# A spectral filter and MLP kernel on one Trainium2 core: compact stage-1 matrices, V reordered first, batch 0's products on three engines, double-matrix blocks for batch 1

## Chip, cores and metric

One core of one Trainium2 chip. The metric is the device time of one execution in microseconds (us); lower is better. Ratios below are of runs in the fast state alone, beside runs of the kernel before on the same chip. Fast runs of one kernel scatter by up to 1.3% (553.67 to 560.84 us for the kernel before in the last rounds), so differences under half a per cent are read with their intervals. The moments inside a kernel come from one profile each.

## The reference

Eight batches of 3136 tokens with 256 channels. A filter over the sequence in the frequency domain, then low-rank token mixing, then an MLP over the channels with a residual:

```python
X = np.fft.rfft(x, axis=1)                        # x: (8, 3136, 256)
y = np.fft.irfft(X * (filt_r + 1j * filt_i), n=3136, axis=1)
# ... y becomes the x of the second part
h = xt @ U @ V                                    # xt = y.transpose(0, 2, 1); U: 3136x32, V: 32x3136
u = y + h.transpose(0, 2, 1)
out = u + np.maximum(u @ w_ch1, 0.0) @ w_ch2      # w_ch1: 256x1024, w_ch2: 1024x256
```

## The kernel before

The transform is factored as 3136 = 64 x 49. **Stage 1** multiplies by 64-point matrices with the twiddles in them (`wf`), **stage 2** by 49-point matrices (`w2t`), then comes the **filter product**, **stage 3** goes back over 49 points (`g3`), and **stage 4** back over 64 points to tokens. Stage 4 has 32 more rows for the low-rank term: V's rows in `sv[64:96]`, and the sum over U's spectrum `uh` copied into `e2[64:96]` by `put_h`. Between stages 1 and 2 and between stages 3 and 4 the data changes its partition axis by a write to and a read from device memory (`ct1`, `ct2`).

TensorE then runs the MLP in groups of 512 tokens, eight steps to a group. The stages 1 to 3 of batch b+1 are laid between these steps by a plan. The **low-rank step** of a batch below is `low_rank(b)`, the sum that `put_h` needs; an **eviction** is the copy of a result out of PSUM, where TensorE leaves it, into SBUF. Only batch 0 has nobody to hide behind. The parts concerned:

```python
wf = cst.tile([128, 25, 128], F16, name="wf")        # two 64-column matrices per block, mostly zeros
# ...
for a in range(0, NK, 8):
    load_filters(a, a + 8)                           # issued by GpSimd
# ...
nc.gpsimd.dma_start(vnat, moe_V)
nc.gpsimd.dma_start(w1sb, ...)

def u_hat():                                         # U's spectrum, on VectorE
    # ...
        for f in range(2):
            nc.vector.tensor_mul(t[f]..., z[...], free(tw, ...))      # z is PSUM
        nc.vector.tensor_add(uh[:, :, p:p + 8], t[0], t[1])           # both inputs in SBUF

def mid_first():                                     # batch 0, stages 2 and 3
    # ...
    for j in range(16):
        # ... stage 2 with w2t and w2t's turned copy: "double-matrix" form, one product instead of three
        if j in (7, 9, 12, 14):
            nc.scalar.copy(pc, pz); nc.gpsimd.tensor_mul(uv, pc, fin)
        else:
            nc.vector.tensor_mul(uv, pz, fin)

def make_fa(i):                                      # filter copies for the later batches' form
    s = slice(8 * i, 8 * i + 8)
    nc.scalar.copy(fc[0:64, s], fb[64:128, s])
    nc.vector.tensor_scalar_mul(fc[64:128, s], fb[64:128, s], -1.0)
    nc.vector.tensor_copy(fa[64:128, s], fb[0:64, s])
    # ...

mid_first()
load_e2(0, 0); load_e2(0, 1)                         # reads of stage 4's input, issued by SyncE
nc.gpsimd.tensor_copy(sv[64:96, :]..., vnat...)      # V reordered
low_rank(0)                                          # 32 matmuls in four column strips
for n, _ in enumerate(st1(1)): ...                   # all 13 pieces of batch 1's stage 1
keep_warm(6)                                         # fillers
stage4(groups[0], 0); stage4(groups[0], 1)
# ...
at(4, x_after, 2)                                    # x loads of batch 2, held until a ReLU of group 0
# ...
m = later(start[b - 1], (5, -9, -12)[min(b, 3) - 1])
z = plan_mid(b, m, (2, 5) if b > 1 else (1, 3, 5))   # blocks whose three products GpSimd does
```

Of the kernel before, what the change touches and what calls it, by code (L numbers as in the profile page):

```python
# [16 lines left out]
NK = 32  # L17
# [7 lines left out]
def _consts():  # L25
# [10 lines left out]
    wf = np.zeros((128, 25, 128))  # L36
    for h in range(2):
        wf[h::2, 0:24, 64 * h:64 * h + 64] = t1[:, 24 * h:24 * h + 24]
    wf[0:64, 24, 0:64] = t1[:, 48]
# [59 lines left out]
    return (wf.reshape(128, 25 * 128).astype(f16), w2.astype(f16), g3.astype(f16),  # L99
# [4 lines left out]
def kernel(  # L104
# [48 lines left out]
    wf = cst.tile([128, 25, 128], F16, name="wf")  # L153
    for c in range(4):
        i = slice(8 * c, min(8 * c + 8, 25))
        nc.sync.dma_start(wf[:, i], wf_d.rearrange("p (i m) -> p i m", m=128)[:, i])
# [47 lines left out]
    usb = hflat[0:64, 0:NR * RANK]  # L204
    nc.gpsimd.dma_start(usb, moe_U.rearrange("(q r) p -> q (r p)", q=NQ))
# [3 lines left out]
    make_identity(nc, idn)  # L209

# [7 lines left out]
    nc.scalar.dma_start(g3, g3_d.rearrange("p (f m) -> p f m", f=6))  # L218

# [4 lines left out]
    vnat = hflat[64:96, 4704:4704 + SEQ]  # L224
    nc.gpsimd.dma_start(vnat, moe_V)
    nc.gpsimd.dma_start(w1sb, moe_w_ch1.rearrange("(h dd) c -> dd h c", h=2))

    sv = cst.tile([96, SEQ], F16, name="sv")
    kr = cst.tile([128, 96], F16, name="kr")

    def keep_warm(n):
        z = bank("f")
        for _ in range(n):
            nc.tensor.matmul(z, wf[:, 0, :], wf[:, 0:4, :].rearrange("p i m -> p (i m)"),
                             start=True, stop=True)
# [4 lines left out]
    def u_hat():  # L240
        ud = hflat[0:64, 1568:4704].rearrange("q (p c r) -> q p c r", c=2, r=NR)
# [18 lines left out]
    def st1(b):  # L260
# [22 lines left out]
        nc.tensor.matmul(pf[0:64, 0:DM], wf[0:64, 24, 0:64], xt[b, 3], start=True, stop=True)  # L283
# [11 lines left out]
    def turned(c):  # L295
        for g in range(0, 8 if c < 3 else 1, 4):
            for hh in range(2):
                z = bank("f")
                n, o = 512, 3136 * hh + (8 * c + g) * 128
                if c < 3:  # L300
                    for i in range(4):
                        nc.tensor.matmul(z[:, 128 * i:128 * i + 128],
                                         xt[0, c][:, (g + i) // 2, DM * (i % 2) + 128 * hh:DM * (i % 2) + 128 * hh + 128],
                                         wf[:, 8 * c + g + i, :], start=(i == 0), stop=True,
                                         skip_group_check=True)
                else:
                    n = 64
                    nc.tensor.matmul(z[:, 0:n], xt[0, 3][:, 128 * hh:128 * hh + 128],
                                     wf[0:64, 24, 0:64], start=True, stop=True)
# [6 lines left out]
    esb = {}  # L316
# [6 lines left out]
    def out3(b, k, half, pe):  # L323
        if half == 0:
            esb[b, k] = sb.tile([98, 4, DM], F16, tag="esb", bufs=10, name="esb")
        nc.scalar.copy(esb[b, k][:, 2 * half:2 * half + 2, :].rearrange("p s d -> p (s d)"),  # L326
                       pe[0:98])
        if half:
# [25 lines left out]
    def mid_first():  # L354
# [18 lines left out]
        todo = []  # L373

        def do3(j, uv):
            pe = bank("e0")
            stage3(pe, [(uv[:, 0], 2, 4), (uv[:, 1], 3, 5)], j == 15)
            out3(0, j // 2, j % 2, pe)

        for k in range(4):  # L380
            turn_a2(k)
        for c in range(4):
            load_x(1, c)
        nc.gpsimd.dma_start(w2sb, moe_w_ch2.rearrange("(cc t) e -> cc (t e)", t=8))
        for j in range(16):
# [7 lines left out]
            if j in (7, 9, 12, 14):  # L393
# [3 lines left out]
                nc.gpsimd.tensor_mul(uv, pc, fin)  # L397
            else:
                uv = sb.tile([128, 2, 2 * DM], F16, tag="ta", bufs=3, name="uv")
                nc.vector.tensor_mul(uv, pz, fin)  # L400
            if j < 4:
                turn_a2(j + 4)
            todo.append((j, uv))
            if len(todo) > 3:
                do3(*todo.pop(0))
        while todo:
            do3(*todo.pop(0))


    h1 = {}  # L410
# [21 lines left out]
    def load_e2(b, c):  # L432
# [5 lines left out]
        nc.sync.dma_start(t[0:64], dram(ct2[b], 8 * c * DM, [[NR * DM, 64], [1, n * DM]]))  # L438
# [19 lines left out]
    def stage4(gr, dh):  # L458
# [23 lines left out]
        nc.vector.tensor_copy(o, v)  # L482
# [58 lines left out]
    def make_fa(i):  # L541
        s = slice(8 * i, 8 * i + 8)
        nc.scalar.copy(fc[0:64, s], fb[64:128, s])
        nc.vector.tensor_scalar_mul(fc[64:128, s], fb[64:128, s], -1.0)
        nc.vector.tensor_copy(fa[64:128, s], fb[0:64, s])
        if i == 3:
# [7 lines left out]
    for c in range(4):  # L554
        turned(c)
        keep_warm(2)
    nc.sync.dma_start(sv[0:64], s4_d)
    nc.sync.dma_start(kr, kr_d)
    mid_first()
    load_e2(0, 0)  # L560
    load_e2(0, 1)
    nc.gpsimd.tensor_copy(sv[64:96, :].rearrange("p (r q) -> p r q", q=NQ),
                          vnat.rearrange("p (q r) -> p r q", q=64))
    low_rank(0)
    for n, _ in enumerate(st1(1)):
        if n == 3:
            low_rank_end(0)
        if n == 6:
            put_h(0, 0)
    load_e2(0, 2)  # L570
    load_e2(0, 6)
    keep_warm(6)
    stage4(groups[0], 0)
    stage4(groups[0], 1)
    for c in (1, 2, 6):
        put_h(0, c)
    make_fa(0)
    make_fa(1)


# [29 lines left out]
    def plan_mid(b, s, on_pool):  # L610
# [36 lines left out]

        lead = (4, 8, 9)[min(b, 3) - 1]
# [3 lines left out]
        for k in range(8):  # L652
            at(s, two, k)
            if k + 3 < 8:
                at(s, fetch, k + 3)
            if k in on_pool:
# [4 lines left out]
            else:  # L661
# [5 lines left out]
                d = max(later(s, 5), end)  # L667
# [29 lines left out]
    gens = {}  # L697

    def step1(b):
        if b not in gens:  # L700
            gens[b] = st1(b)
        next(gens[b])

    for c in range(3, 6):
        at(8 * c - 14, load_e2, 0, c)
    at(1, make_fa, 2)
    at(3, make_fa, 3)
# [7 lines left out]
    for b in range(1, NB):  # L715
# [4 lines left out]
        m = later(start[b - 1], (5, -9, -12)[min(b, 3) - 1])  # L720
        z = plan_mid(b, m, (2, 5) if b > 1 else (1, 3, 5))
# [46 lines left out]
```

## Time and profile before

555.93 us (median of 3, 555.91 to 557.05); profiled span 555.2 us.

| marker in the profile before | us |
|---|---|
| first filter product | 25.1 |
| last stage-3 eviction of batch 0 | 49.1 |
| first stage 4 / first MLP matmul of group 0 | 59.5 / 61.2 |
| first MLP matmul of group 1 | 72.0 |
| low-rank step of batch 1 | 121.1 |
| low-rank step of batch 2 | 183.3 |

Later batches follow about every 61 us. The time can therefore be split at three markers: the **start** (to group 1), the **middle** (group 1 to batch 1's low-rank step), the **handoff** (from there to batch 2's low-rank step). A change there moves the end by as much.

Five lines of the timeline of the kernel before will be needed (start, length, engine, line, operation, output and input, count, idle before and its releaser; SPq is SyncE issuing transfers):

```profile
12.48 0.42 DVE L257 TENSOR_TENSOR uh<-ut 98x256 f16<-98x256 f32 x1
...
47.44 6.95 POOL L562 COPY sv<-hring 32x3136 f16<-32x3136 f16 x1
...
59.59 1.05 SPq L286 DMA_DIRECT2D ct<-al  x1
...
66.92 0.60 PE L352 MATMUL psum<-a,w2t 98*128 98x512 f16 x2
67.02 4.25 POOL L170 DMA_DIRECT2D x<-in_x_dram  x6 [0.33 <-POOL x L168]
```

Read them as an order of events. U's adds (0.42 us) are long over when GpSimd reorders V. Batch 1's last stage-1 write (`al`) goes out at 59.6 us, its first stage-2 block runs at 66.9 without a wait, and the x loads of batch 2 start only after that.

### The profile page before, as it was taken

The numbers are of one execution on the slowest core, as the hardware profiler recorded it, in microseconds if no ns is written. First come the engines' busy times: TensorE is split into PE (matmuls) and PEld (weight loads), VectorE is DVE, ScalarE is ACT, GpSimd is POOL, SyncE is SP. The second block draws the span as 40 slices with busy tenths as digits, with TensorE's granted clock in tenths as the row PEclk, the third lists the DMA queues.
The fourth block names the chain that finished last, engine by engine and source line by source line (L and its number), as shares of the span: only waits on it lengthen the run. The fifth ranks groups of instructions, "written<-read, shape, count | busy, mean of one in ns | idle before, by whom it ended". The sixth has DMA issues, their size and how long they took to land.

```text
span 555.2 us, 11638 instructions
## 1 busy us (share of the span) xinstructions
PE 517.2 (93%) x4491; PEld 375.3 (68%) x4491; DVE 353.1 (64%) x409; ACT 390.8 (70%) x684; POOL 282.4 (51%) x194
## 2 busy tenths in 40 slices
PE   5976689997999999999999999999999999999996
PEld 2634356664767777777776777777786777777775
DVE  6764675755756686758846785858746887643332
ACT  8566868774777688767776788677777577765663
POOL 5778179951883165915683175806563297300000
PEclk9999899997999999999999999999999999999999
DMA  9998876894669468774879468865653553333212
GB/s 194 157 170 192 225 141 187 209 230 130 174 184 250 125 176 199 173 204 137 193 222 221 123 173 228 166 199 152 186 170 121 141 167 121 106 113 115 96 77 87
DMA packets 85432, 92.06 MB, mean 166 GB/s; under 512 B 6741, under 2 KB 69416, under 8 KB 85376
## 3 DMA queue, kind: packets, MB, share of 16 engines
q1 hardware_dynamic: 67968, 75.12, 45.5%
q0 software_dynamic: 16960, 15.91, 19.1%
q8 instruction: 35, 0.57, 0.4%
q10 hardware_dynamic: 448, 0.28, 0.3%
q14 instruction: 21, 0.17, 0.1%
HBM read 57.42 MB, written 49.77 MB: 193 GB/s over the span
## 4 chain that ended last, share of the span: by engine, by line
PE 70%; POOL 10%; DVE 7%; DMA 6%; ACT 4%; issue 2%; DVEq 0%; ACTq 0%; POOLq 0%; SPq 0%
PE psum L521 25%; PE psum L488 24%; PE psum L352 4%; PE psum L344 4%; PE psum L477 4%; PE psum L497 3%; PE psum L266 3%; POOL y L634 3%; DMA x<-in_x_dram 3%; POOL x L170 2%; DVE ut L482 1%; DVE tb L632 1%; PE psum L416 1%; DMA w1sb<-in_moe_w_ch_dram 1%; ACT asb L273 1%
## 5 line engine op out<-in xcount | busy, mean ns | idle before, releaser
L492 ACT ACTIVATE hring<-psum 128x512 f16<-128x512 f32 (+1 forms) x416 | 237.7, 576 | 104.5 <-PE psum L488 103.2
L488 PE MATMUL psum<-ut,w1sb 128*128 128x512 f16 (+1 forms) x832 | 240.3, 370 | 6.4 <-ACT hring L492 3.0
L521 PE MATMUL psum<-w2sb,hring 128*128 128x256 f16 x1536 | 230.9, 273 | 0.0
L634 POOL TENSOR_TENSOR y<-ta,tb 128x1024 f16<-128x1024 f16 x56 | 120.5, 2159 | 159.4 <-DVE tb L632 115.5
L521 PEld LDWEIGHTS <-hring 128*128 128x128 f16 x1536 | 143.3, 98 | 63.8 <-issue 3.8
L482 DVE CAST ut<-psum 128x512 f16<-128x512 f32 x96 | 71.1, 741 | 108.3 <-PE psum L477 88.2
L488 PEld LDWEIGHTS <-w1sb 128*128 128x128 f16 x832 | 104.6, 145 | 27.3 <-issue 10.4
L529 DVE COPY och<-psum 128x512 f32<-128x512 f32 x96 | 66.2, 689 | 47.3 <-PE psum L497 46.6
L326 ACT CAST esb<-psum 98x512 f16<-98x512 f32 x128 | 74.7, 586 | 21.6 <-PE psum L344 16.0
L628 DVE TENSOR_TENSOR ta<-psum,fb 128x1024 f16<-128x1024 f32 x41 | 50.0, 1218 | 7.9 <-PE psum L352 6.9
L273 ACT CAST asb<-psum 128x512 f16<-128x512 f32 x78 | 45.7, 589 | 12.3 <-PE psum L266 11.2
L497 PE MATMUL psum<-idn,ut 128*128 128x128 f16 x392 | 54.0, 220 | 0.0
L477 PEld LDWEIGHTS <-e 96*128 96x128 f16 x768 | 35.9, 99 | 25.5 <-issue 10.2
L630 DVE TENSOR_TENSOR tb<-psum,fc 64x1024 f16<-64x1024 f32 x41 | 50.3, 1226 | 0.9
L632 DVE TENSOR_TENSOR tb<-psum,fc 64x1024 f16<-64x1024 f32 x41 | 49.9, 1218 | 0.8
L477 PE MATMUL psum<-sv,e 96*128 96x64 f16 x768 | 38.8, 194 | 6.5 <-DMA e<-ct 3.7
L344 PE MATMUL psum<-y,g 128*98 128x512 f16 x105 | 39.9, 380 | 3.0 <-POOL y L634 1.5
L497 PEld LDWEIGHTS <-ut 128*128 128x128 f16 x392 | 38.4, 98 | 4.9
L628 POOL TENSOR_TENSOR ta<-pc,fb 128x1024 f16<-128x1024 f16 x15 | 32.4, 2159 | 10.7 <-ACT pc L638 10.7
L352 PE MATMUL psum<-a,w2t 98*128 98x512 f16 x113 | 34.3, 379 | 1.7 <-DVE tb L632 1.6
L266 PE MATMUL psum<-x,wf 128*128 128x256 f16 x168 | 31.3, 274 | 2.8 <-DVE asb L271 1.0
L630 POOL TENSOR_TENSOR tb<-pc,fc 64x1024 f16<-64x1024 f16 x15 | 31.8, 2122 | 1.2
(93 smaller groups left out, 373.6 us busy)
## 6 DMA issues: line engine op xcount, KB each, us to landing
out_dram<-och SPq DMA_DIRECT2D x47, 512.0 KB
ct<-esb SPq DMA_DIRECT2D x64, 196.0 KB
x<-in_x_dram POOLq DMA_DIRECT2D x48, 256.0 KB, 8.1
e<-ct SPq DMA_DIRECT2D x48, 256.0 KB
a<-ct SPq DMA_DIRECT2D x56, 196.0 KB
ct<-asb SPq DMA_DIRECT2D x42, 256.0 KB
wf<-wf SPq DMA_DIRECT2D x3, 256.0 KB
w1sb<-in_moe_w_ch_dram POOLq DMA_DIRECT2D x1, 512.0 KB, 6.8
```

Source lines behind the costliest of these rows:

```text
L326: nc.scalar.copy(esb[b, k][:, 2 * half:2 * half + 2, :].rearrange("p s d -> p (s d)"), pe[0:98])
L344: nc.tensor.matmul(pe[0:98], g3[:, m, :], v, start=(n == 0), stop=(n == len(parts) - 1))
L477: nc.tensor.matmul(pu[:, 64 * i:64 * i + 64], e2[b, c][:, i, 128 * dh:128 * dh + 128], sv[:, 64 * r:64 * r + 64], start=(i == 0), stop=Tru ...
L482: nc.vector.tensor_copy(o, v)
L488: nc.tensor.matmul(ph[:, 0:n], w1sb[:, dh, :, t], gr.ut[:, dh, 0:n], start=(dh == 0), stop=(dh == 1))
L492: nc.scalar.activation(h[:, 0:n], ph[:, 0:n], RELU)
L497: nc.tensor.matmul(o[:, dh * 128:dh * 128 + 128], gr.ut[:, dh, t0:t0 + n], idn, start=False, stop=(dh == 1), skip_group_check=True)
L521: nc.tensor.matmul(o, gr.h[tt][:, i * 128:(i + 1) * 128], w2sb[:, tt, :], start=(tt == 0), stop=False, skip_group_check=True)
L529: nc.vector.tensor_copy(gr.och[:, 2 * y:2 * y + 2, :].rearrange("p j d -> p (j d)"), gr.pc)
L628: eng.tensor_mul(ta, p, va)
L630: eng.tensor_mul(tb[0:64], p[64:128], vb[64:128])
L634: nc.gpsimd.tensor_add(ys[k], ta, tb)
```

## The change

The intent: shorten the start, where batch 0 has nobody to hide behind, and the handoff to batch 1. The core of the diff:

```diff
-    wf = np.zeros((128, 25, 128))                    # table halved, unpacked on VectorE
+    wf = np.zeros((128, 25, 64))
 ...
+    vnat = hflat[64:96, 0:2 * SEQ].bitcast(F32)
+    nc.scalar.dma_start(vnat, moe_V)
+    sv = cst.tile([96, SEQ], F16, name="sv")
+    nc.gpsimd.tensor_copy(sv[64:96, :].rearrange("p (r q) -> p r q", q=NQ),
+                          vnat.rearrange("p (q r) -> p r q", q=64))
     for a in range(0, NK, 8):
         load_filters(a, a + 8)
 ...  in mid_first: products, stage 3 and the low-rank sum in a new order
+            while whole:
+                low_rank_part(whole.pop(0))          # four matmuls at a time, one column strip
+                if k == 6:
+                    load_e2(0, 0, 48, 0)             # 48 rows ahead of the last write
+                if k == 7:
+                    load_e2(0, 0, 64, 48)
-            if j in (7, 9, 12, 14):
+            if j in on_pool:                         # (5, 8, 11); w1, x and w2 loads between them
 ...
-    keep_warm(6)
-    stage4(groups[0], 0)
-    stage4(groups[0], 1)
+    for _ in range(8):                               # 8 of 13 stage-1 pieces; five more in group 0
+        step1(1)
+    for dh in range(2):
+        stage4(groups[0], dh)
 ...
-        nc.scalar.copy(fc[0:64, s], fb[64:128, s])
+        nc.vector.tensor_copy(fc[0:64, s], fb[64:128, s])
 ...  in plan_mid: blocks 0, 1, 7 of batch 1 in double-matrix form
+                if k == 1:
+                    at(later(s, 6), make_fa, 0, 8)   # planes 0 to 8 only now
 ...
-        m = later(start[b - 1], (5, -9, -12)[min(b, 3) - 1])
-        z = plan_mid(b, m, (2, 5) if b > 1 else (1, 3, 5))
+        m = later(start[b - 1], (8, -9, -12)[min(b, 3) - 1])
+        z = plan_mid(b, m, (2, 5) if b > 1 else (2, 4), () if b > 1 else (0, 1, 7))
```

## The prediction

> **What bounds the kernel now.** I read the page's busy line and its slices first, then the busy times of chosen stretches, the chain of work that ended last, the waits of TensorE, and last the timeline of the first 140 us. The page says who is full and when:
>
> ```profile
> PE 517.2 (93%) x4491; PEld 375.3 (68%) x4491; DVE 353.1 (64%) x409; ACT 390.8 (70%) x684; POOL 282.4 (51%) x194
> PE   5976689997999999999999999999999999999996
> PEclk9999899997999999999999999999999999999999
> ```
>
> PE is at nine tenths from the sixth slice on; what it loses lies in the first ten slices (139 us), where the granted clock also dips twice. The stretches give the loss in us (columns: stretch, its length, busy PE, PEld, DVE, ACT, POOL with counts, clock, DMA share, GB/s):
>
> ```profile
> 0.00:61.20 61.20, 44.95 (x312) 26.55 (x313) 36.77 (x45) 41.14 (x47) 39.91 (x50) 0.94 0.99 186
> 61.20:72.04 10.84, 5.70 (x42) 3.15 (x39) 9.79 (x18) 7.78 (x10) 4.97 (x8) 1.00 0.88 198
> 126.40:136.00 9.60, 5.48 (x37) 3.61 (x38) 5.52 (x7) 1.97 (x4) 0.00 (x0) 0.64 0.43 106
> 183.00:245.00 62.00, 61.38 (x542) 45.26 (x540) 43.32 (x48) 46.07 (x83) 33.98 (x21) 1.00 0.70 182
> ```
>
> From 183 us each batch costs about 61 us of filled TensorE; nothing there is touched, so it can only move as a whole. The change can win in three places: the start up to the first MLP matmul (61.2 us), token group 0 (61.2 to 72.0 us, 5.1 us idle), and the handoff to batch 1 (126.4 to 136 us: 4.1 us idle, and the rest at clock 0.64). The start, from the timeline (start, length, engine, line, count, idle before and its releaser):
>
> ```profile
> 38.77 0.59 PE L344 MATMUL psum<-uv,g 128*98 128x512 f16 x2 [2.46 <-POOL uv L397]
> 57.00 3.69 ACT L543 COPY fc<-fb 64x2048 f16<-64x2048 f16 x2
> 57.03 2.72 PE L234 MATMUL psum<-wf 128*128 128x512 f16 x6 [0.45 <-ACT al L285]
> 64.30 0.69 DVE L545 COPY fb<-fb 64x2048 f16<-64x2048 f16 x1
> 66.01 1.07 PE L488 MATMUL psum<-ut,w1sb 128*128 128x512 f16 x4 [1.46 <-ACT hring L492]
> ```
>
> Here GpSimd's product comes 2.5 us late, ScalarE spends 1.85 us on a filter copy that VectorE does in 0.69, ReLUs stand behind those copies, and six filler matmuls delay the first real one. The handoff, from the chain of work that ended last:
>
> ```profile
> 119.76 6.48 DMA ct<-esb
> 126.38 3.58 DMA e<-ct
> 130.09 0.60 PE psum L477 x8
> ```
>
> Batch 1's last stage-3 tile leaves at 119.8 us, and a write and a read through HBM take 10 us, while TensorE has work for only 6.6 us of them.
>
> **What the Trainium skill says.** "TensorE: Matmul & The Clock Gate", Part 1 (the HAM clock gate): an idle window of about 3.4 us halves the clock, and a busy one restores it. The trace agrees: after the 3.7 us wait, the pairs of 512-column matmuls take 1.06 us instead of 0.60 until about 135 us. "DMA: Bandwidth & Descriptors", Anatomy of one DMA: about 2 us per transfer are fixed, most of it the write receipt; the two legs of 6.5 and 3.6 us are above that, with the DMA share at 1.09 from 113 to 121 us. "VectorE: DVE Perf Modes", Mode 4x_2P: a 16-bit copy inside SBUF may make four results a cycle; the trace has 2048 columns in 0.69 us (about 3 a ns), against 512 columns from PSUM in 0.69 us. "GPSIMD Engine Reference", section 1: its SBUF interfaces are shared with VectorE's two-port instructions. One filter copy took 0.83 instead of 0.69 us as GpSimd's x issue began, which settles nothing.
>
> **The change, part by part.**
>
> *Compact matrices.* The packed table is 410 KB instead of 819 KB, and the 0.4 MB synthesis table is loaded later; the float32 U and V add about 0.4 MB of reads. DMA is full (share 1.03) in the first 20 us, so x should land up to 1 us sooner. But VectorE must unpack (two multiplies of 1536 columns, at the filter scale's 0.69 us per 2048 some 0.5 us each), and the ten warm-up matmuls now read a region whose memset ends at 6.1 us. They start there instead of at 3.5 us and last 4.4 us, to 10.5 us; U's spectrum, which started on TensorE at 9.0, starts 1.4 us later, and VectorE's 6 us of it end at 17.3 instead of 15.9. Then six or seven evictions of 0.69 us: 21.6 us for the stage-1 turn, as before (21.5). Worth nothing.
>
> *V first.* The GpSimd copy of 6.95 us leaves 47.4 us, where nobody waited for it, for a place ahead of all filter loads. GpSimd stood idle much of 9 to 19 us, waiting on DMA lanes. I take V to land at 9, the copy to end at 16, and 21 filter issues of 0.585 us to end at 28.3 us (27.9 before). First filters then land near 22.5 us, ahead of the first product at about 24.7 (25.1 before; only three transposed blocks stand ahead of it, not four). Neutral, with a risk.
>
> *Batch 0 on three engines.* Products on GpSimd fall from four to three (L400's twelve become thirteen on VectorE) and start at 32 instead of 36.6 us, as the weight loads move behind them. Thirteen products of 1.23 us and one eviction of 0.69 make 16.7 us from 24.7; I add 2 us for the one product that GpSimd delivers late (its issues of 2.6 us stand between the first and second). Last product 43.5, last stage-3 eviction 45.3 us; before 49.1. **Gain 3.8.** The low-rank sum (1.06 us) is spread between and loses its use of four column strips; it hides in TensorE's slack.
>
> *Eight of thirteen stage-1 pieces, no filler.* The last write goes out at 46.1, lands by 49.3 (49.2 to 52.45 before, the same), 16 rows come back by 51.5; the pieces are done by 50. First stage 4 at 51.5 instead of 59.5, first MLP pair at 54 instead of 62.2 us. **Gain 8 so far.**
>
> *Group 0.* ScalarE is rid of 4 x 1.87 us. VectorE gets them at 4 x 0.69, and has between the two halves of group 1's input: an unpacking of h 0.68, two stage-1 evictions 1.38, copies for planes 8 to 24 of 2 x 2.1, h 0.9, two evictions 1.46. That is 8.6 us, and with waits for the two stage-1 pieces about 10, so group 1 starts at 64 instead of 72.0 us. **The gain stays 8.0**: VectorE takes ScalarE's place as the bound of this stretch.
>
> *Batch 1.* Stage 1 now ends at about 61 us (57 before), four to five plan steps later; its writes (0.6 to 1 us of issue each), their landing and the read take another 6 to 7 us, so the first stage-2 block at step 8 should wait 2 us where 0.7 was idle. **Loss 1.4.** Blocks 0, 1 and 7 in double-matrix form cost TensorE 12 more matmul-equivalents of 0.215 us, 2.6 us, and a stage 2 of 0.43 us that used to lie before group 1 lies after it. **Loss 3.0.** They save VectorE 1.23 us and GpSimd 2.13 us a block, and one block fewer goes to GpSimd (8.5 us). By the plan's arithmetic the middle stage ends at step 39 of 48 instead of 41. Two steps are about 2.2 us; GpSimd freed earlier also takes the x loads out of the last write's way, an estimated 2 us of its 6.5. Of the 4.1 idle and 2.0 half-clock us, 0.5 remain. **Gain 5.6.** GpSimd's late sum at 114.5 us (0.8 us) and some of ScalarE's queue at 90 to 100 us (1.45 us, I take 0.4) go too. **Gain 1.2.**
>
> Sum: 8.0 - 1.4 - 3.0 + 5.6 + 1.2 = 10.4 us, so 555.9 - 10.4 = **545.5 us**.
>
> **Rivals.** (a) The start gains but the handoff does not: batch 0 is consumed eight us earlier while batch 1's middle stage starts three steps later in the plan (8 instead of 5). If its first block waits long for stage 1's round trip through HBM, everything shifts, the 9 steps of slack are eaten, and the clock halves again. For it: VectorE's crowded queue in group 0, and SP's issues in order. Against it: the four-step pooled block is gone and GpSimd has some 27 us of work where it had 41. Result 550 to 552 us. (b) V ahead of the filters makes filter landing the bound of the start: V at 12, copy to 20, first product 27 us, with GpSimd's products late as well and TensorE at half clock. Result 548 to 550 us. (c) All goes smoothly: GpSimd's products arrive in time, last stage-3 eviction at 43, no wait for batch 1's first block, no handoff wait. Gains of 2 + 2 + 0.5 more: 541 us. (d) The double blocks' 2.6 us of TensorE eat the gain: only if the handoff wait was hidden already, which the 3.7 us wait speaks against.
>
> **Range and chances.** The start is uncertain by about 2.5 us, the step after it by 2, the handoff by 2; together some 4. 80% range 540 to 551. The 2% line lies at 544.8 us, just under my figure; the parts look tuned to each other, which favours (c) a little. Faster by over 2%: 0.46; within: 0.52; slower: 0.02.
>
> **What would show it.** Right: first stage-4 matmul near 51.5 us, first MLP pair near 54, group 1 near 64; no 3.7 us DMA wait at the handoff and no clock dip there; batches still 61 us apart afterwards. Wrong in the start: the first filter product after 26 us, or waiting for a filter DMA. Wrong in group 0: TensorE held by ScalarE there. Wrong in batch 1: over 3 us of wait at its first stage-2 block, or a DMA wait left at the handoff. The prediction fails most likely through GpSimd's queue in the start or the round trip of batch 1's stage 1.

## The result

The changed kernel takes **573.35 us** (median of 4, 572.55 to 575.67) against 556.49 for the kernel before in the same rounds: ratio 1.0291, 95% interval 1.0226 to 1.0355. It is slower by almost 3%, and correct. Here and below a ratio is the mean time of one kernel's fast runs over that of the other's of the same rounds, so it is not quite the ratio of the medians quoted.

The slices of the page, after (40 equal parts of the span; TensorE's busy share and, below, the share of its full clock that it was granted, both in tenths):

```profile
PE   4588619799799999999999999999999999999996
PEclk9599758999999999999999999999999999999999
```

Read against the same two lines of before. In the second slice (14 to 29 us) TensorE falls from 9 tenths to 5, and its clock from 9 to 5; in the sixth (72 to 86 us) from 8 tenths to 1, with a clock of 5 and then 8. The clock dip of before in the tenth slice is gone, but the eleventh is at 7 tenths instead of 9. From the twelfth on nothing has changed. The markers say where the time went:

| marker | before | predicted | after |
|---|---|---|---|
| first filter product | 25.1 | 24.7 | 30.3 |
| last stage-3 eviction of batch 0 | 49.1 | 45.3 | 55.0 |
| first stage 4 | 59.5 | 51.5 | 61.5 |
| group 1 | 72.0 | 64.0 | 74.8 |
| low-rank step of batch 1 | 121.1 | - | 138.9 |
| low-rank step of batch 2 | 183.3 | - | 199.8 |

By stage (differences of the rows): start +2.8 instead of -8.0; middle +15.0 (64.1 us instead of 49.1) instead of +3.2 (1.4 + 3.0 - 1.2 in the prediction); handoff -1.3 (60.9 instead of 62.2) instead of -5.6. The sum, 16.5, is the difference of the two profiled spans (571.9 - 555.2 = 16.7).

The timeline of the changed kernel has both large losses in it:

```profile
11.86 0.43 DVE L267 TENSOR_TENSOR uh<-ut 98x256 f16<-98x256 f32 x1
...
13.24 5.73 POOL L232 CAST sv<-hring 32x3136 f16<-32x3136 f32 x1 [6.97 <-DMA hring<-in_moe_V_dram]
13.31 5.95 DVE L267 TENSOR_TENSOR uh<-ut 98x256 f16<-98x256 f32 x1
...
69.79 4.35 POOL L177 DMA_DIRECT2D x<-in_x_dram  x6 [0.30 <-POOL x L175]
72.20 1.06 SPq L296 DMA_DIRECT2D ct<-al  x1
```

An add that took 0.43 us before and after it takes **5.95 us** when it starts 0.07 us after GpSimd's reordering of V; it ends at 19.26, 0.29 us after the copy. And batch 1's last stage-1 write goes out at 72.2 us, when six x loads of batch 2 have been going out since 69.8. What that costs is in the chain of work that ended last (start, length, what), and in TensorE's waits. The chain:

```profile
72.20 9.91 DMA ct<-al
82.37 2.86 DMA a<-ct
```

The waits of TensorE (us in total, times, longest), of which this is the costliest row:

```profile
PE psum L364 <- DMA a<-ct: 9.5, 2, 9.0
```

A write of 32 KB (64 rows of 256 values of 2 bytes) takes 9.9 us, and TensorE stands 9.0 us. In the kernel before the order was the other one: write at 59.6, x loads at 67.0. The x loads hang on a ReLU of group 0 and moved by 2.8 us, the write by 12.6. The stretches around it (length, busy PE, PEld, DVE, ACT, POOL with counts, clock, DMA share, GB/s):

```profile
76.00:85.30 9.30, 0.26 (x3) 0.03 (x1) 0.09 (x1) 0.02 (x1) 0.00 (x0) 0.50 0.99 192
85.30:95.00 9.70, 9.52 (x49) 5.45 (x49) 4.88 (x5) 3.46 (x6) 0.00 (x0) 0.70 0.32 83
...
199.90:261.90 62.00, 61.35 (x540) 45.26 (x539) 43.66 (x48) 46.03 (x84) 34.05 (x21) 1.00 0.73 182
```

For 9.3 us every engine stands while the DMA is full; then TensorE is busy for 9.7 us at clock 0.70. The last line shows that a later batch is as it was.

Two smaller events of the same kind as the add are in the timeline further on. In VectorE's row, two of the three filter copies of planes 0 to 8 beside GpSimd's products (0.69 us each when alone):

```profile
108.32 2.52 DVE L585 TENSOR_SCALAR fc<-fb 64x2048 f16<-64x2048 f16 x1
110.87 2.50 DVE L586 COPY fb<-fb 64x2048 f16<-64x2048 f16 x1
```

And a `put_h` copy at the handoff beside a GpSimd add, with the TensorE wait that follows behind VectorE's queue:

```profile
144.07 2.12 POOL L669 TENSOR_TENSOR y<-ta,tb 128x1024 f16<-128x1024 f16 x1 [15.79 <-DVE tb L667]
144.64 2.10 DVE L485 COPY e<-h 32x2048 f16<-32x2048 f16 x1
...
148.69 0.39 PE L518 MATMUL psum<-sv,e 96*128 96x64 f16 x8 [1.38 <-DVE ut L523]
```

**The theory.** Two collisions make the loss: VectorE is locked out by a GpSimd instruction wherever it reads SBUF twice or copies quickly inside SBUF, and the x loads hold up batch 1's stage-1 write. **The rivals**: V's late landing or the filter loads behind it delay the start; VectorE or SyncE makes batch 1's stage 1 late; the double-matrix blocks cost too much.

### The profile page after: what moved, and what is told of

It is laid out like the page before. It is cut to its first block, busy times and chain, and to the rows that moved or that the text cites. A ratio compares the mean times of both kernels' runs of the same rounds, so it can differ in the third digit from the quotient of the medians.

```text
span 571.9 us, 11642 instructions
## 1 busy us (share of the span) xinstructions
PE 521.1 (91%) x4498; PEld 377.3 (66%) x4498; DVE 368.0 (64%) x419; ACT 382.5 (67%) x678; POOL 266.6 (47%) x185
## 4 chain that ended last, share of the span: by engine, by line
PE 73%; DVE 8%; POOL 5%; DMA 5%; ACT 5%; issue 2%; SPq 0%; ACTq 0%; POOLq 0%; DVEq 0%
PE psum L562 25%; PE psum L529 25%; PE psum L364 5%; PE psum L356 4%; PE psum L518 4%; PE psum L538 3%; PE psum L276 3%; POOL y L669 2%; DMA ct<-al 2%; DMA a<-ct 1%; DVE tb L667 1%; DVE uh L267 1%; PE psum L456 1%; ACT asb L283 1%; ACT hring L533 1%
## 5 line engine op out<-in xcount | busy, mean ns | idle before, releaser
L669 POOL TENSOR_TENSOR y<-ta,tb 128x1024 f16<-128x1024 f16 x53 | 114.8, 2170 | 160.7 <-DVE tb L667 123.6
L562 PEld LDWEIGHTS <-hring 128*128 128x128 f16 x1536 | 143.6, 98 | 65.7 <-issue 5.9
L518 PEld LDWEIGHTS <-e 96*128 96x128 f16 x768 | 35.9, 98 | 26.1 <-issue 11.1
L663 DVE TENSOR_TENSOR ta<-psum,fb 128x1024 f16<-128x1024 f32 x39 | 47.5, 1219 | 7.1 <-PE psum L364 6.6
L665 DVE TENSOR_TENSOR tb<-psum,fc 64x1024 f16<-64x1024 f32 x39 | 47.8, 1226 | 0.8
L667 DVE TENSOR_TENSOR tb<-psum,fc 64x1024 f16<-64x1024 f32 x39 | 47.5, 1218 | 0.8
L663 POOL TENSOR_TENSOR ta<-pc,fb 128x1024 f16<-128x1024 f16 x14 | 30.7, 2194 | 34.4 <-ACT pc L673 34.4
L364 PE MATMUL psum<-a,w2t 98*128 98x512 f16 x118 | 36.5, 387 | 10.7 <-DMA a<-ct 9.5
L356 PE MATMUL psum<-y,g 128*98 128x512 f16 x100 | 38.0, 380 | 2.2 <-ACT esb L337 1.1
L177 POOL DMA_DIRECT2D x<-in_x_dram x48 | 31.3, 665 | 1.1 <-POOLq L819 0.8
```

Source lines behind the costliest of these rows:

```text
L356: nc.tensor.matmul(pe[0:98], g3[:, m, :], v, start=(n == 0), stop=(n == len(parts) - 1))
L364: nc.tensor.matmul(pz, w, a, start=True, stop=True)
L518: nc.tensor.matmul(pu[:, 64 * i:64 * i + 64], e2[b, c][:, i, 128 * dh:128 * dh + 128], sv[:, 64 * r:64 * r + 64], start=(i == 0), stop=Tru ...
L562: nc.tensor.matmul(o, gr.h[tt][:, i * 128:(i + 1) * 128], w2sb[:, tt, :], start=(tt == 0), stop=False, skip_group_check=True)
L663: eng.tensor_mul(ta, p, va)
L669: nc.gpsimd.tensor_add(ys[k], ta, tb)
```

## Experiments

### The two collisions, one at a time and together

**v_late**: the reordering moved behind batch 0's products.

```diff
-    nc.gpsimd.tensor_copy(sv[64:96, :]..., vnat...)   # ahead of load_filters
     ...
     mid_first()
+    nc.gpsimd.tensor_copy(sv[64:96, :]..., vnat...)
```

> The changed kernel with the GpSimd reordering of V moved back behind batch 0's filter products (V itself is still loaded early). Theory, shared SBUF port: the second add of U's spectrum on VectorE falls from 5.95 to 0.43 us, the first filter product starts near 25 instead of 30.3 us, the whole takes 568 us (573.4 less 5). Rival, the add was slow through the full DMA or something else of that stretch: it stays at several us, and the time stays at 573.

Measured 568.6 us, ratio 1.0223 (1.0185 to 1.0261). From its timeline, the add that took 5.95 us and the first product:

```profile
13.68 0.43 DVE L265 TENSOR_TENSOR uh<-ut 98x256 f16<-98x256 f32 x1
...
25.03 1.23 DVE L437 TENSOR_TENSOR uv<-psum,fb 128x1024 f16<-128x1024 f32 x1 [1.04 <-PE psum L362]
```

All four adds take 0.42 to 0.43 us, and group 1 comes at 69.5 instead of 74.8. The order of the reordering alone is worth 5.3 us of the start.

**v_pieces**: the reordering stays where it is, in seven instructions instead of one.

```diff
-    nc.gpsimd.tensor_copy(sv[64:96, :]..., vnat...)
+    for i in range(7):
+        nc.gpsimd.tensor_copy(sv[64:96, 448 * i:448 * i + 448]..., vnat...[:, 7 * i:7 * i + 7])
```

> The changed kernel with the same GpSimd reordering of V at the same place, but in 7 pieces of 448 columns (0.8 us each). Theory, a GpSimd instruction keeps the port until it ends and VectorE gets its turn between two: each add of U's spectrum waits at most 0.9 us, the first filter product starts at 26 to 28 us, the whole takes 569 to 571 us. Rival, GpSimd's reads as a whole go first: one add still waits over 5 us, 573 us.

Measured 574.02 us, 1.0311 (1.0275 to 1.0346). From its timeline:

```profile
12.49 7.05 POOL L233 CAST sv<-hring 32x448 f16<-32x448 f32 x7 [6.21 <-DMA hring<-in_moe_V_dram]
13.01 0.73 DVE L268 TENSOR_TENSOR uh<-ut 98x256 f16<-98x256 f32 x1
...
14.79 0.98 DVE L268 TENSOR_TENSOR uh<-ut 98x256 f16<-98x256 f32 x1
```

The copy's total (7.05 us) and its place are as before, yet the adds now last 0.73 to 1.00 us. So VectorE waits for the end of one GpSimd instruction, of 1 us here and 5.7 us there; V's landing and the filters behind it are not what held the add. The expected 569 to 571 us were missed, as the time was not gained: the first product came at 26.4 us (1.4 us of it a wait for a filter transfer, so the cause that rival (b) of the prediction names comes next), but the read of group 0's input was waited for 5.7 us instead of 2.8, and the stage-1 write was still slow. This shows the mechanism, and that a gain in the start can be lost at the next wait.

**x_gated**: batch 2's x loads wait for batch 1's first stage-2 input.

```diff
-            load_x(b, c, groups[0].h[3] if c == 0 else None)
+            load_x(b, c, first_a2[0] if c == 0 else None)
 ...
-    at(4, x_after, 2)
+    at(7, x_after, 2)
```

> The changed kernel with batch 2's x loads held until batch 1's first stage-2 input has landed. Theory, these 3.2 MB of reads stand in the way of stage 1's last write: that write lands within 4 us instead of 9.9, TensorE waits at most 3 us instead of 9.0 at batch 1's first block and its clock doesn't halve there; a new wait for x of up to 3 us may come at batch 2's first stage-1 matmul; 564 to 569 us. Rival, the write is slow by its own small packets or SP's order: the 9 us stay, 573 us or more.

Measured 567.09 us, 1.0183 (1.0140 to 1.0226). Two lines of its chain:

```profile
71.52 3.23 DMA ct<-al
75.01 2.81 DMA a<-ct
```

The same write, issued at the same time, lands in 3.2 instead of 9.9 us; TensorE waits 2.5 instead of 9.0. The middle falls from 64.1 to 57.5 us. One part of the expectation missed: the clock halved all the same (0.50 from 73 to 82 us).

**v_late_x_gated**: both.

> Both edits in the changed kernel. If the two waits are independent, the gains add: 558 to 563 us. If the second only moves with the first (the start earlier, but the next wait longer), 565 us or more. Neither theory expects it to beat the kernel before (556) by over 2%.

Measured 561.42 us, 1.0101 (1.0069 to 1.0133): within the noise the gains add (6.8 and 10.8 thousandths of the ratio alone, 19.0 together). Group 1 comes at 69.1 us, batch 1's low-rank step at 126.6, batch 2's at 187.5. This **repaired kernel** is the base of the next runs. It is still 1% slower than the kernel before, with a middle of 57.6 us (49.1) and a handoff of 60.9.

**old_v_first**: the reverse test, V first in the kernel before.

```diff
+    nc.gpsimd.dma_start(vnat, moe_V)
+    nc.gpsimd.tensor_copy(sv[64:96, :]..., vnat...)
     for a in range(0, NK, 8):
         load_filters(a, a + 8)
```

> The kernel before with one part of the change alone: V's load and its GpSimd reordering (here float16 to float16, 6.95 us where it stood) go ahead of the filter loads. Port theory (VectorE's two-input adds inside SBUF wait for the end of a GpSimd instruction): one of the four adds of U's spectrum, 0.43 us before, lasts 3 to 6 us beside the copy; the first filter product comes at 28 to 30.5 us instead of 25.1, and the kernel takes 4 to 5.5 us longer, about 561 us (ratio 1.007 to 1.010). Rival, that only the filter loads are delayed behind the copy: the adds keep 0.43 us, and the first product waits for a filter DMA. Rival, that it needs the new kernel's other start (float32 V, compact matrices): adds keep 0.43 us, no change of the time.

Measured 566.34 us, 1.0181 (1.0129 to 1.0233), and my theory's numbers missed: all four adds keep 0.43 us. In this kernel V is loaded by GpSimd itself, behind the x loads, and lands at 20.5 us, after the adds; GpSimd waits 11.4 us for it, and the filter loads stand behind. The first product waits 8.9 us for a filter:

```profile
34.04 3.55 DVE L402 TENSOR_TENSOR uv<-psum,fb 128x1024 f16<-128x1024 f32 x3 [8.91 <-DMA fb<-in_filt_i_dram]
```

The rival named there is right: V first costs the start either way, by the lock if V lands early and by the filters if it lands late. The lock itself was not tested in this kernel, as no add met the copy.

### What still holds the repaired kernel

None of the six correct runs of this part can be told from the base by its total: their ratios are 1.0057 to 1.0098, and every interval overlaps the base's (1.0069 to 1.0133). What follows compares moments of one profile each. These profiles differ already at the first product (23.2 to 25.8 us), before any of the edits acts, so a moment is best counted from an earlier marker of its own profile.

**fa_late**: the filter copies of planes 0 to 8 after the middle stage.

```diff
-                if k == 1:
-                    at(later(s, 6), make_fa, 0, 8)
                 if k == 7:
                     at(later(s, 1), make_fa, 28, 32)
+                    at(later(s, 3), make_fa, 0, 8)
```

> On top of both edits: the filter copies for planes 0 to 8 moved from beside GpSimd's first product of batch 1 to the end of batch 1's middle stage, where GpSimd has little. Theory, shared port: the three copies take 0.7 us each instead of 1.1, 2.5 and 2.5, and TensorE's two waits of 1.3 and 1.9 us for the next group's input go; 558 to 559.5 us (2 to 3 less). Rival, the waits there come from ScalarE's queue: 561 us.

Measured 560.33 us, 1.0057 (1.0031 to 1.0083). The copies take 0.69 us each; the middle falls by 2.0 us to 55.5, but the handoff grows by 1.5 to 62.4. In one profile each, the gain is given back by the next wait; the expected 558 to 559.5 us were missed.

**lr_end**: the low-rank sum of batch 0 in one piece with four column strips, as before the change.

```diff
-            while whole:
-                low_rank_part(whole.pop(0))
 ...
+    low_rank(0)
+    low_rank_end(0)
     put_h(0, 0)
```

> On top of both edits: batch 0's low-rank sum back in one piece behind the products, in four column strips (the form of the kernel before). Theory, the 32 matmuls in one strip and their waits for ScalarE fill TensorE during the products: the last stage-3 eviction comes 2 to 3 us earlier (49.8 now), the sum costs 1.6 us behind it, and the whole gains 0.5 to 1.5 us. Rival, ScalarE and VectorE set the pace of the products: last eviction within 0.7 us of 49.8, the whole 1 to 2 us longer.

Measured 561.02 us, 1.0068 (1.0045 to 1.0092). Batch 0's last stage-3 eviction ends at 44.9 us instead of 49.5. Of these 4.6 us, 1.7 are only an earlier first product (23.2 against 24.9 us): from first product to last eviction it takes 21.7 instead of 24.7 us, so the edit gains 3.0. First stage 4 gains only 1.3 us (54.6), since the read of its input is waited for 5.2 us instead of 2.7.

**lr_end_k7**: the same, with the last stage-3 write issued ahead of the read.

```diff
-                if k == 6:
-                    load_e2(0, 0, 48, 0)
                 if k == 7:
-                    load_e2(0, 0, 64, 48)
+                    load_e2(0, 0)
```

> As lr_end (both repairs, low-rank sum in one piece), and group 0's input is read in one load of 64 rows that SyncE issues after the last of batch 0's stage-3 writes, instead of 48 rows ahead of that write. Theory that SyncE's order held the last write back (issued 49.5 us with its data ready at 44.4): the last write goes out by 46 us, the read lands at 51.5 to 52.5, first stage 4 at 52 instead of 54.6 us; about 2.5 us less than lr_end if it survives the handoff, 557 to 559 us. Rival, that the full DMA (share 1.1 to 1.18 from 30 to 45 us) sets the landing: the writes land late all the same, first stage 4 after 54 us, time as lr_end (561).

Measured 560.72 us, 1.0088 (1.0063 to 1.0112). The last write leaves by 46.8 us, and still the read can be issued only at 51.0, with first stage 4 at 54.63 us, as in lr_end. But the first product came 1.6 us later than there: counted from the last eviction, first stage 4 comes after 8.2 us, against 9.8 in lr_end and 8.7 in new_best (below), which has lr_end's order. So SyncE's order may be worth 0.6 to 1.6 us, and the larger part of the wait remains for the rival, the full DMA.

**asb_act**: batch 1's last stage-1 chunk evicted by ScalarE alone.

```diff
-                if b == 1 and j % 2:
+                if b == 1 and j % 2 and c < 2:
```

> On top of both edits: the last chunk of batch 1's stage 1 is evicted by ScalarE alone, so that it doesn't stand in VectorE's queue behind the filter copies. Theory, VectorE's queue delays stage 1's last write: it goes out 1.5 to 2 us earlier than 66.6 us, TensorE's wait at batch 1's first block falls from 2.4 to under 1 us, and group 1 starts up to 1.4 us earlier; 557 to 559 us. Rival, SP's issues set that time: the write stays within 0.5 us and the time at 561.

Measured 560.66 us, 1.0069 (1.0048 to 1.0090). The write of `al` goes out at 66.3 us (66.6 in the base), which looks like the rival. But this profile's first stage 4 came 0.8 us later: counted from there, the write comes after 9.6 instead of 10.7 us. Nor was SyncE busy issuing: in the base it waits 5.5 us between its fourth and its fifth write, for the third chunk. The chunk's last matmul was done at 62.9 us, and its last eviction stood in VectorE's queue behind the filter copies:

```profile
63.19 0.69 DVE L584 COPY fb<-fb 64x2048 f16<-64x2048 f16 x1
...
64.55 0.66 DVE L279 CAST asb<-psum 128x512 f16<-128x512 f32 x1
...
65.28 1.25 SPq L285 DMA_DIRECT2D ct<-asb  x2
```

So VectorE's queue does hold the write, by about 1.1 us. Group 1 starts sooner too (11.1 instead of 13.2 us after first stage 4), TensorE's wait at the first block grows to 4.0 us, and the total shows no gain. The theory's delay is there, at 1.1 instead of 1.5 to 2 us, and nothing of it reaches the end.

**single_blocks**: no double-matrix blocks for batch 1; GpSimd takes blocks 1, 3, 5 as before the change.

```diff
-        z = plan_mid(b, m, (2, 5) if b > 1 else (2, 4), () if b > 1 else (0, 1, 7))
+        z = plan_mid(b, m, (2, 5) if b > 1 else (1, 3, 5))
 ...
-    at(7, make_fa, 24, 28)
+    at(6, make_fa, 0, 8)
+    at(7, make_fa, 24, 32)
```

> On top of both edits: batch 1 without double-matrix blocks (three blocks on GpSimd as before the change, all filter copies done in group 0). Prediction's theory, the double blocks cost TensorE 2.6 us and buy more than that at the handoff: without them a DMA wait of 2 to 4 us comes back at the handoff to batch 2's tokens and the time is 563 to 566 us. Rival, they buy nothing here: 557 to 560 us.

Measured 570.09 us, 1.0235 (1.0197 to 1.0273). The result is wrong (error 0.138), because the middle stage now ends so late that a `put_h` copy falls behind the stage 4 that reads it (by the plan's arithmetic at step 47, where that stage 4 stands at 46 and 47); the work is the same. TensorE waits 11.1 us in three times for stage 4's input. This is 4 us above the expected range. The run moves two sets of filter copies into group 0 as well, so it supports that the double blocks buy more than they cost, and does not measure by how much.

**fill**: ten filler matmuls ahead of batch 1's first stage-2 block.

```diff
+        def fill(n):
+            for _ in range(n):
+                nc.tensor.matmul(psum[:, 5], wf[:, 0, :], ..., start=True, stop=True)
 ...
+                    if (b, k, half) == (1, 0, 0):
+                        at(s, fill, 10)
                     at(s, two_q, k, half)
```

> As v_late_x_gated, with ten filler matmuls of 512 columns (0.215 us each at full clock) on TensorE just ahead of batch 1's first stage-2 block, where it waits 2.4 us and then runs at clock 0.53 for 6 us. Theory that the half clock is caused by this wait and costs some 2.9 us: granted clock above 0.9 from 73 to 79 us, the low-rank step of batch 1 1.5 to 3 us earlier, total 558.5 to 560 us if the handoff keeps it. Rival, that the clock had been lowered by the idle shares of group 0 before it, so the fillers come too late: clock below 0.7 as before and the time the same or up to 2 us longer.

Measured 561.01 us, 1.0076 (1.0035 to 1.0117). The clock from 76 to 82 us is 1.00 instead of 0.79, the middle falls by 2.4 us to 55.2, and the handoff grows by 1.6 to 62.5, with a clock of 0.79 from 133 to 140 us. Again a gain that the next stage takes. The half clock does not begin in the wait that was filled: in the base it lasts from 68.3 to 78.6 us and begins while TensorE waits 3.3 us for group 1's input; with the fillers it ends at 72.1. So the wait for the first block prolongs the half clock and does not start it.

**fill_put**: the `put_h` copies of batch 1's groups 1 and 2 one plan step later.

```diff
-                at(l, put_h, b, c)
+                at(later(l, 1) if b == 1 else l, put_h, b, c)
```

> As fill (both repairs and ten filler matmuls ahead of batch 1's first block), with batch 1's copies put_h of groups 1 and 2 one plan step later, so that the first no longer starts while GpSimd adds (in fill it took 2.11 us beside an add that ended 1.4 us after its start, and the two stage-4 evictions behind it came late: TensorE waited 1.38 and 1.77 us). Theory of a third port collision: the copy takes 0.68 us, the two waits together fall below 1.5 us, the clock does not dip at 137 us, and the low-rank step of batch 2 comes at 184 to 186 us instead of 187.2; total 558 to 559.5 us. Rival, that VectorE has simply more to do there than TensorE: the copies cost their time one step later, low-rank step of batch 2 within 0.7 us of 187.2, total as fill (561).

Measured 561.03 us, 1.0098 (1.0061 to 1.0136). The edit missed its target: no VectorE instruction lies between the two places, so the copy of group 1 kept its place in VectorE's order, began 0.57 us into GpSimd's add, and took 2.11 us again. It decides nothing; the next runs repeat it.

### The repairs together

**new_best**: the repaired kernel with fill, fill_put, fa_late and lr_end.

> All repairs of the changed kernel together: V reordered behind batch 0's products, x loads of batch 2 gated, the low-rank sum in one piece, the first filter copies after the middle stage, the fillers, and put_h one step later. If the gains add where they did not before because the next wait took them: low-rank step of batch 2 at 182 to 184 us, total 555 to 557.5 us, the same as the kernel before. Rival, that the chain from batch 1's stage 1 through its writes and reads to the handoff takes each gain back: total 559 to 561 us.

Measured 558.14 us, 1.0043 (1.0023 to 1.0063), between the two expectations: middle 53.3, handoff 61.9 us.

**new_put2**: the same, `put_h` two steps later.

```diff
-                at(later(l, 1) if b == 1 else l, put_h, b, c)
+                at(later(l, 2) if b == 1 else l, put_h, b, c)
```

> As new_best, with batch 1's put_h copies of groups 1 and 2 two plan steps later, which puts the first behind VectorE's next product and so nearly behind GpSimd's add (in new_best it took 2.11 us beside an add that ended 1.56 us after its start). Third port collision: the copy takes 0.7 to 1.1 us, the stage-4 evictions come about 1.1 us earlier, TensorE's two waits on them fall from 1.39 and 1.07 by about that together or in part, low-rank step of batch 2 at 183 to 184 us instead of 184.4, total 557 to 557.8 us. Rival, VectorE has as much to do as before and the evictions stay: low-rank step within 0.3 us of 184.4 and no change.

Measured 556.06 us, 1.0004 (0.9980 to 1.0027). Of its timeline:

```profile
128.68 2.12 POOL L669 TENSOR_TENSOR y<-ta,tb 128x1024 f16<-128x1024 f16 x1 [15.60 <-DVE tb L667]
...
130.43 0.92 DVE L477 COPY e<-h 32x2048 f16<-32x2048 f16 x1
```

The copy starts near the end of the add and takes 0.92 instead of 2.11 us. TensorE's wait for the second stage-4 half falls from 1.39 to 0.26 us, the clock stays at 1.00, and the handoff from 61.9 to 59.2 us. The middle is 1.3 us longer in this profile (with a 1.0 us wait for a stage-2 read), so batch 2's low-rank step is 1.6 us earlier (182.7). The third collision is real, and moving the copy out of it is worth 2.7 us of the handoff in one profile each; the totals come from different rounds, and their intervals just overlap.

**new_w2**: also, the load of the second weight matrix held until group 0's stage-4 input has landed.

```diff
-                if j == 8:
-                    nc.gpsimd.dma_start(w2sb, ...)
 ...
+    nc.gpsimd.tensor_copy(w2sb[0:1, 0, 0:1], e2[0, 0][0:1, 0, 0:1])
+    nc.gpsimd.dma_start(w2sb, ...)
```

> As new_put2, and the load of the second weight matrix (0.5 MB in the tile, 8.6 us to land, issued at 40.4 us) is held back on GpSimd until group 0's stage-4 input has landed. If the full DMA holds batch 0's last stage-3 writes and the read after them: the read lands 2 to 4 us earlier, first stage 4 at 52 to 54 us instead of 56.0, group 1 up to 2 us earlier, and a total of 555 to 557 us, the same as the kernel before or just under. Rival, that batch 1's stage-1 writes and reads then run into the held-back load (it lands at about 59 us, those writes go out from 56 us): first block not earlier than 73 us, total as new_put2 or longer.

Measured **553.40 us**, ratio 0.9920 (0.9892 to 0.9947): 0.8% faster than the kernel before, and better than expected. new_put2 was timed in the same rounds (556.06), and the intervals don't overlap. Its timeline:

```profile
51.01 0.62 POOL L592 DMA_DIRECT2D w2sb<-in_moe_w_ch_dram  x1 [0.32 <-POOL w2sb L591]
...
52.87 0.39 PE L508 MATMUL psum<-sv,e 96*128 96x64 f16 x8 [1.61 <-DMA e<-ct]
...
65.66 0.58 PE L519 MATMUL psum<-ut,w1sb 128*128 128x512 f16 x1 [3.29 <-DVE ut L513]
```

The read is waited for 1.6 instead of 4.1 us, and group 1 starts at 65.7 us instead of 68.9. Start, middle and handoff are 65.7, 53.5 and 59.2 us: -6.4, +4.4 and -3.0 against before, in sum -4.9 (rounded before adding) for a span that is 4.8 us shorter.

### The kernel before, improved in place

**old_trim**: no fillers ahead of stage 4, and filter copies on VectorE.

```diff
-    keep_warm(6)
 ...
-        nc.scalar.copy(fc[0:64, s], fb[64:128, s])
+        nc.vector.tensor_copy(fc[0:64, s], fb[64:128, s])
```

> The kernel before with two cuts in the start and nothing else: the six filler matmuls ahead of the first stage 4 are dropped (2.7 us on TensorE just ahead of it), and the filter copies for the later batches' first operand go from ScalarE (3.69 us for two) to VectorE (0.69 each). If the start of the kernel before is bound there: first stage 4 at 57 instead of 59.5 us, group 1 2 to 4 us earlier, and a total of 552 to 554 us (ratio 0.993 to 0.997). Rival: the first stage 4 waits for the read of its input or for VectorE anyway, or the gain is given back by a longer DMA wait at the handoff to batch 1 (3.7 us now): 555 to 557 us.

Measured 558.79 us, 1.0043 (1.0021 to 1.0064). First stage 4 comes at 57.1 us, 2.4 earlier, but TensorE waits 4.6 us for batch 1's first stage-2 input, and the low-rank steps of batches 1 and 2 are where they were (121.1, 183.25). The profiled run took 556.98 us, less than the median, so its markers do not show what the slower runs lost.

**old_trim_gated**: the same with x_gated's edit.

> As old_trim (no fillers ahead of the first stage 4, filter copies on VectorE), with the x loads of batch 2 held back until batch 1's first stage-2 input has landed. In old_trim they were issued from 64.1 us, as the read of that input was (64.3), and TensorE waited 4.6 us. Theory that the collision took the gain: wait below 2.5 us, first block at 66 to 67 us instead of 68.7, low-rank step of batch 2 1 to 2.5 us before 183.25, total 553.5 to 555.5 us. Rival, that the gain is lost at the handoff (3.8 us read of stage-4 input) whatever the start does: first block earlier, low-rank step of batch 2 within 0.5 us, total 556 to 559 us.

Measured 559.03 us, 1.0050 (1.0017 to 1.0083). The wait falls to 2.4 us and the first block comes at 65.7 instead of 68.65, and still nothing is gained: the clock is 0.68 from 52 to 70 us and 0.55 from 70 to 76 us, where it is 0.91 and 1.00 in the kernel before. The six fillers that I had counted as a pure cost seem to pay for themselves; no run took them out alone.

**old_fill**: twelve fillers at the handoff's wait.

```diff
+            if n == 5 and t == 6:
+                for _ in range(12):
+                    nc.tensor.matmul(psum[:, 4], wf[:, 0, :], ..., start=True, stop=True)
```

> The kernel before with twelve filler matmuls of 512 columns ahead of batch 1's first stage 4 at the handoff, in the 3.7 us that TensorE waits for its input (12 x 0.215 = 2.6 us). The prediction put the half clock after this wait at 2.0 us. If so: clock above 0.9 from 130 to 136 us, low-rank step of batch 2 1.2 to 2 us before 183.3, total 554 to 555 us. Rival, that VectorE (evictions, put_h copies and a product) sets the pace there: clock kept up but the low-rank step less than 0.7 us earlier, total as before (556).

Measured 556.07 us (median of 22 runs, two of them slow), 0.9995 (0.9968 to 1.0022). The fillers ran from 124.6 to 127.4 us, a wait of 2.3 us was left, and the clock was halved all the same, from 131 to 138 us. So neither expectation was tested, and what the half clock costs the kernel before stays open.

## Why the prediction was wrong, step by step

- **"which settles nothing"** is the step that failed first. Only the transfer issue beside one filter copy was looked at; V's reordering was moved beside VectorE's work on U without asking what that work reads. The table row that the prediction took from "GPSIMD Engine Reference", section 1, names instructions with two SBUF inputs too, and the prediction left that half out. The Trainium skill has the full rule on a page that I had not opened: "SBUF — State Buffer", section Who interferes with whom, says that VectorE and GpSimd share one port pair as an exclusive lock held for a whole instruction, and names two-input VectorE instructions against a GpSimd one that reads SBUF. The trace agrees: 5.95 instead of 0.43 us, 0.73 to 1.00 beside pieces of 1 us, and multiplies with one input in PSUM not held up. The V step was called neutral and cost 5.3 us. Rival (b) had the place right, and its cause wrong: the copy landed at 13.2 and ended at 19.0 us, about as (b) had it, but no product waited for filters (in v_pieces, without the long lock, the first did, for 1.4 us).
- **"the first stage-2 block at step 8 should wait 2 us"**: the mechanism, the trip through device memory, was right, and the term mis-sized: 9.0 us. Stage 1 ended 9.3 us after first stage 4, as predicted (51.5 to 61), and SyncE issued its writes in 0.6 to 1.2 us each. But the "6 to 7 us" for writes, landing and read became 14.4 us (70.8 to 85.2), because the x loads, which the sum of this step did not hold at all, came 2.4 us before the last write. With them out of the way (x_gated) the trip took 7.7 us and the wait 2.5 us, close to what was predicted. x_gated puts the collision at 6.6 us of the middle. Rival (a) had this wait and the halved clock in it, with 550 to 552 us instead of what came.
- **"no filler" as a gain**: without the fillers, and with the waits of group 0, TensorE runs at half clock before and behind the wait; fill wins 2.4 us of the middle back. It was in no term of the sum.
- **"VectorE gets them at 4 x 0.69"**: the filter copies take that when alone; planes 0 to 8 took 1.1 to 2.5 us beside GpSimd's products. fa_late puts it at 2.0 us.
- **The middle closes, if these three add**: +15.0 measured; 6.6 (x loads) + 2.4 (clock) + 2.0 (copies) leave 4.0, where 3.2 was predicted. The kernels with all three repairs keep a middle 4.2 to 5.6 us longer than before. The 3.0 us of extra TensorE work were not measured alone; single_blocks supports that the double blocks buy more than they cost.
- **Batch 0's products**: from first product to last stage-3 eviction 20.6 us were predicted (24.7 to 45.3). It took 24.0 us before, 24.7 as written, and 21.7 with the low-rank sum in one piece (lr_end and every run built on it). So the spread sum cost more than the new order gained, and even without it the gain is 2.3 of the predicted 3.4 us. The sum does not hide "in TensorE's slack"; four matmuls take about 0.6 us in one strip, and TensorE was busy for 22.9 of the 25.7 us of this stretch. In lr_end and its successors it takes 1.06 us in one piece.
- **"The last write goes out at 46.1, lands by 49.3 (49.2 to 52.45 before, the same)"**: it did not, since w1, w2 and x loads were moved into just these microseconds. lr_end and lr_end_k7 gave 54.6 us for first stage 4, new_w2 52.9, against 51.5 predicted and 59.5 before. The DMA's fill at 30 to 50 us was in the profile of before (share 0.99 up to 61 us), and I did not count it against the path.
- **Handoff**: the DMA wait of 3.7 us and its clock dip did go, as predicted. In their place VectorE was behind, through the locked `put_h` copy: -1.3 us instead of -5.6, and -3.0 in new_put2 and new_w2.
- **Right** without repair: compact matrices worth nothing (no run needed them to explain anything, and none tested them alone), 10 us from first MLP pair to group 1 (64.3 to 74.8), warm-up from 6.1 us, and later batches at their old pace.

So the first half of the prediction, a start of 64 us, was within 1.7 us of the best start of these runs (65.7); the change as written kept three pairs of things side by side that must not be. Left open: the missing 2.6 us of the handoff, and why the trimmed starts cost 0.4% in the kernel before, where the profile of old_trim, of one of its faster runs, shows equal low-rank steps.

## What to carry to other kernels

Before moving a GpSimd instruction, list what VectorE does in that time: two-input operations and fast copies inside SBUF wait for its end, so long GpSimd instructions belong beside VectorE work that reads PSUM. A small write on the critical path needs the bulk loads behind it, not in front, and a load nobody needs yet can be gated on the arrival of the one that is needed. A gain in one stage counts only if the next wait does not take it: read the markers after every stage, and repair the waits in the order of time.

## What the Trainium skill lacked or had wrong

- "SBUF — State Buffer", Who interferes with whom: nothing wrong; the lock showed as stated in three places. What it does not give is the loss when GpSimd runs instruction after instruction: beside back-to-back products, VectorE copies of 0.69 us took 2.5 us each, and GpSimd's own went from 2.12 to 2.45 and 2.57 us.
- "GPSIMD Engine Reference", section 1, states the sharing in one table row (which does name two SBUF inputs) without saying that the loser waits for the whole instruction. That row alone reads like a slowdown; it was a factor of 14 (5.95 against 0.43 us).
- "DMA: Bandwidth & Descriptors", Anatomy of one DMA, gives the fixed cost of a transfer, there for those that GpSimd issues, and neither it nor the rest of the page lets one size a small write under load: SyncE's 32 KB took 9.9 us behind x loads and 3.2 us without them.
- "TensorE: Matmul & The Clock Gate", Part 1: the window named there for a halved clock is idle, and about 3.4 us. In these runs a window did not have to be idle throughout: the clock halved at 131.0 us in old_fill after 3.4 us in which TensorE was busy for 1.4 us, its longest wait being 2.3 us. The remark on micro-idles further on in Part 1 gives no figure either.
